# Sparse attention and a balanced mixture of experts on one core: the planner's durations, the first expert's w2 scale, and the sums of x

## The chip, the core and the metric

One core of one Trainium2 chip runs the whole program in one launch. The metric is the device time of one execution in microseconds, as a median of several runs. PE is the matmul engine (TensorE), DVE VectorE, ACT ScalarE, POOL GpSimd, and SP only issues DMAs. Each engine executes its own instructions in the order in which the program holds them; an instruction that waits holds up everything behind it on its engine.

## What is computed

```python
# attention: 4 batches x 8 heads, 768 positions, head size 64, block mask
scores = where(mask, q @ k.T / sqrt(64), -1e9); attn = softmax(scores); y = attn @ v
# x = y as [3072, 512]; 8 experts, w1 [8, 512, 1024], w2 [8, 1024, 512]
logits = x @ w_gate; P = exp(logits - logits.max())
for _ in range(8):
    P /= P.sum(1, keepdims=True) + 1e-9
    P /= P.sum(0, keepdims=True) + 1e-9
    P *= 3072 / 8
for e in range(8):
    out += P[:, e:e+1] * (relu(x @ w1[e]) @ w2[e])
```

## The kernel before

**Attention.** A table says after which of 192 tiles (one head, one 128-row column of keys) each step is issued; the order in it is kept on every engine. Batch 3 is the last. The first expert's w1 is loaded, scaled and split during attention. The load of the first w2 is issued at tile 184, and its scale is made at the very end of the table: eight sums of magnitudes on ACT (`magnitude`, L329), a maximum on DVE (L415), one transpose on PE that spreads it over the partitions (L335), and six short DVE steps (L421 to L428). The last two groups of transposes of the attention output (`turn_x`, L970) stand behind that PE transpose.

**Experts.** All 8 experts run over 4 batches, 32 rounds; round i is expert i // 4 and batch i % 4. A matmul of f32 accuracy is three f16 matmuls of high and low parts, so every operand is split: a high part by ACT and a low part by DVE or POOL. Both matrix products of a round use a seven-product (Strassen-like) scheme, p = 0 to 6. `stage1` multiplies by w1 (PE, L1546, 6 matmuls of 384 columns for each of four f-chunks of a product p), takes the results out of PSUM with ACT (L1528) and DVE (L1519), and forms the seven hidden operands h with POOL (L1784), ACT (L1746, L1761) and DVE or POOL (low parts, L1752 and L1750; L1767 on DVE). `stage2` multiplies by w2 (PE, L1866) and adds into acc with DVE (L1902). PE takes stage2 of round i and stage1 of round i + 1 in turn.

For the products p in `TWO = (6, 3, 1)` a second level of the scheme is used from expert 1 on (`inner_product`, L1575): 7 groups of 6 matmuls of 192 columns in place of 4 groups of 6 matmuls of 384. It needs sums of quarters of w1 (`inner` in `fetch_w1`, made on POOL L1299, ACT L1357, DVE L1362) and sums of quarters of x. The latter are made once for each batch and p, 12 times in all, by `prep_x`: load, add high and low part (L1482), four subtractions (L1491), split again (L1498, L1503), store to DRAM as `xsd`. Before, they are created in rounds 0 to 3, expert 0, and `closed[0]`, which every later use of the sums waits for, comes after the last of them.

**The planner.** `Plan` simulates the expert part before the program is emitted: each job has engines with durations, dependencies, buffers that it takes and drops, and a due time `dl` worked back from the jobs that need it. A job that may run on DVE or POOL goes to whichever the simulation would finish earlier. The simulation multiplies durations on ACT, DVE and POOL by `MARGIN`. What it yields is only an order: the program is emitted in the order in which the jobs start in the simulation, and semaphores do the rest. `balance` makes the eight normalisations of P: 8 chains of DVE steps (L1239 to L1260) with a PE matmul (L1250) in each.

**Memory.** `xfp` and `xst` (the f32 copy of x for odd batches, and four staging tiles) live in a 24 KB region until `close_late` releases it as a whole and the sums are put there.

Of the kernel before, what the change touches and what calls it, by code (L numbers as in the profile page):

```python
# [20 lines left out]
P = 128  # L21
# [14 lines left out]
SLK, SLK2, SHIFT, EASE = 1.5, 2.0, 8.0, 0.3  # L36
# [16 lines left out]
class Job:  # L53
    __slots__ = (
        "engs", "fn", "deps", "take", "drop", "pt", "dl", "stream", "kb",
        "rush", "wait", "succ", "start", "end", "eng", "ready", "seq", "free",
# [3 lines left out]
class Plan:  # L60
    LAT = 0.2
    DMA_RATE, DMA_LAND = 190.0, 2.0
    MARGIN = 1.06
# [21 lines left out]
    def job(self, engs, fn, deps=(), take=(), drop=(), pt=None, dl=None, stream=None, kb=0, rush=False):  # L85
# [7 lines left out]
        j.rush = rush  # L93
# [30 lines left out]
    def run(self):  # L124
# [3 lines left out]
        dma_free = 0.0  # L128
        items = {p: [(0.0, t) for t in ts] for p, ts in self.shelf.items()}
# [42 lines left out]
        def start(j, e, t):  # L172
            nonlocal dma_free, left
# [12 lines left out]
            else:  # L186
                j.end = t + dur
                free[e] = j.end
            if e == "-":
                free[e] = 0.0  # L190
# [7 lines left out]
            for s in j.succ:  # L198
                s.wait -= 1
                if not s.wait:  # L200
# [3 lines left out]
                    )  # L204
# [6 lines left out]
        while left:  # L211
            moved = False
            for e in ENG:
                while free[e] <= t + EPSI:
# [5 lines left out]
                    for j in mine:  # L220
                        if j.ready <= t + EPSI and allowed(j, t) <= t + EPSI:
# [33 lines left out]
            nxt = [free[e] for e in ENG if free[e] > t + EPSI]  # L255
            nxt += [j.ready for j in cand if j.ready > t + EPSI]
# [19 lines left out]
def tile_sparse_attention_moe(  # L276
# [79 lines left out]
    def scale_power(tag, s, inv, top):  # L356
# [10 lines left out]
    late = ExitStack()  # L367
    xfp, xst = (
        late.enter_context(tc.tile_pool(name=nm, bufs=n, side="right", reuse_waits="tile"))
        for nm, n in (("xfp", 1), ("xst", 4))  # L370
# [9 lines left out]
    def carve(at, dtype, *shape, home=arena):  # L380
# [9 lines left out]
        )  # L390

# [112 lines left out]
    def x_split(b, nm, at_):  # L504
        src = quads_of(b)[at_]
        st = xst.tile([P, 2, KH, TH], F16, tag="xs", name=f"xs_{b}_{nm}")
# [61 lines left out]
    with ExitStack() as actx:  # L568
# [18 lines left out]
        masks = xfp.tile([P, 2, S], BF16, tag="xf", name="masks")  # L587
# [377 lines left out]
        def turn_x(n, c0):  # L965
# [9 lines left out]
            if hp == 0 and c0 == 0:  # L975
                xfs[b] = (xfp if b % 2 else xfa).tile([P, KD, NC, P], F32, tag="xf", name=f"xf_{b}")
# [155 lines left out]
    sums = {}  # L1132

    shelf["xs"] = [xst.tile([P, 2, KH, TH], F16, tag="xs", name=f"stage_{n}") for n in range(4)]
# [12 lines left out]
    def ascend(b):  # L1147
# [21 lines left out]
        def plain(k):  # L1169
# [17 lines left out]
            pe = job({"PE": 1.0}, mm, los, take=(bk,), drop=free)  # L1187
# [33 lines left out]
    def balance(deps):  # L1221
# [9 lines left out]
        pe = job({"PE": 0.3}, spread, (d,), take=(b0,))  # L1231
# [5 lines left out]
        for it in range(8):  # L1237
            d = seq([
                ("DVE", 0.35, lambda: V.tensor_reduce(out=rs, in_=pw, axis=AX.X, op=ALU.add)),  # L1239
                ("DVE", 0.33, lambda: V.tensor_scalar(rs, rs, EPS, None, ALU.add)),  # L1240
# [10 lines left out]
                (d,), take=(bk,),  # L1251
# [7 lines left out]
                ("DVE", 0.29, lambda: V.tensor_scalar(cs, cs, CAP, None, ALU.mult)),  # L1259
# [13 lines left out]
    def scale_jobs(which, e, loaded):  # L1273
# [17 lines left out]
        pe = job({"PE": 0.3}, spread, (whole,), take=(bk,))  # L1291
# [31 lines left out]
    def fetch_w1(e):  # L1323
# [12 lines left out]
        d_s3 = tts(s3, q00, q10, KH, base, 1.3)  # L1336
        d_s1 = tts(q10, q10, q11, KH, tuple(d_s3), 1.35, ALU.add)
# [6 lines left out]
        def inner(p, src, deps):  # L1344
            if p not in TWO:
# [12 lines left out]
                (d, closed[0]) + tuple(used1.get((e - 1, p, "in"), ())),  # L1358
            )
            lo = job(  # L1360
                {"DVE": 1.5},
# [13 lines left out]
        d_s2 = tts(q00, q10, q00, KH, tuple(out[0]) + tuple(d_s1), 1.35)  # L1375
        put(5, q00, d_s2)
        d_s4 = tts(q00, q01, q00, KH, tuple(out[5]), 1.35)
# [7 lines left out]
    def fetch_w2(e, loaded=None, done=None):  # L1385
# [8 lines left out]
        if loaded is None:  # L1394
            loaded = raw_load(2, e)
# [15 lines left out]
        d_t1 = tts(t1, m01, m00, h2, base, 0.85)  # L1411
        one = put(1, m10, base)
        zero = put(0, m00, d_t1)
        d5 = tts(m00, m11, t1, h2, tuple(zero), 1.05)
        five = put(5, m00, d5)
        d6 = tts(m01, m01, m11, h2, tuple(d_t1), 1.05)
        six = put(6, m01, d6)
        d3 = tts(m10, m10, m00, h2, tuple(one) + tuple(d5), 1.05)
# [31 lines left out]
    def load_x(i):  # L1450
# [6 lines left out]
        if i >= B:  # L1457
            for p in TWO:
# [4 lines left out]
                        deps + (closed[0],),  # L1463
# [3 lines left out]
    def prep_x(i):  # L1467
        b = i % B
        for p in TWO:
# [11 lines left out]
                {"DVE": 0.95, "POOL": 2.1},  # L1481
# [6 lines left out]
            for o, x, y in ((0, 1, 0), (1, 3, 1), (3, 3, 0), (2, 2, 3)):  # L1488
                last = job(
                    {"DVE": 0.36, "POOL": 0.75},  # L1490
# [22 lines left out]
                384, (lo,), drop=(st,),  # L1513
# [18 lines left out]
    def stage1(i, t0, length):  # L1532
        e, b = divmod(i, B)
        two = TWO if e else ()
# [142 lines left out]

        got = {}
        if two:
            got[6] = inner_product(6)  # L1680
            got[3] = inner_product(3, got[6])
            got[1] = inner_product(1)

        for g in range(NF // 2):
# [3 lines left out]
            if two:  # L1688
                R, U, C = got[1][0][g], got[6][0][g], got[3][0][g]
                rdep, udep, cdep = (  # L1690
                    [x for k in range(2) for x in got[p][1][g, k]] for p in (1, 6, 3)
                )
                t_r = t_u = t_c = ()
            else:
                R, U, C = (hold("pair") for _ in range(3))
# [19 lines left out]
            if two:  # L1715
                for q, (j, end) in outer(0, X, True, {}).items():
                    r_[q] = scaled_add(cell(R, q), bank(X[q]), cell(R, q), [j] + rdep, dl=end + SLK)
                for q, (j, end) in outer(5, X, False, {q: (r_[q],) for q in qis}).items():
                    c_[q] = scaled_add(cell(C, q), bank(X[q]), cell(C, q), [j] + cdep, dl=end + SLK)
                for q, (j, end) in outer(4, X, False, {q: (c_[q],) for q in qis}).items():  # L1720
                    u_[q] = scaled_add(cell(U, q), bank(X[q]), cell(U, q), [j] + udep, dl=end + SLK)
            else:
                Z = {q: hold("s1") for q in qis}
                Y = {q: hold("s1") for q in qis}
                first = lambda t, q: (t,) if q == qis[0] else ()
                k0, k5, k6 = {}, {}, {}
                for q, (j, end) in outer(0, X, True, {}).items():
                    k0[q] = scaled_copy(cell(R, q), bank(X[q]), (j,), take=first(R, q), dl=end + SLK)
                for q, (j, end) in outer(1, Z, True, {}).items():
                    r_[q] = scaled_add(cell(R, q), bank(Z[q]), cell(R, q), (j, k0[q]), drop=(Z[q],), dl=end + SLK)  # L1730
                for q, (j, end) in outer(5, X, False, {q: (k0[q],) for q in qis}).items():
                    k5[q] = scaled_copy(cell(C, q), bank(X[q]), (j,), take=first(C, q), dl=end + SLK)
                for q, (j, end) in outer(6, Y, True, {}).items():
                    k6[q] = scaled_copy(cell(U, q), bank(Y[q]), (j,), take=first(U, q), dl=end + SLK)
                for q, (j, end) in outer(4, X, False, {q: (k5[q],) for q in qis}).items():
                    u_[q] = scaled_add(cell(U, q), bank(X[q]), cell(U, q), (j, k6[q]), dl=end + SLK)
                for q, (j, end) in outer(3, Y, False, {q: (k6[q],) for q in qis}).items():
                    c_[q] = scaled_add(cell(C, q), bank(Y[q]), cell(C, q), (j, k5[q]), drop=(Y[q],), dl=end + SLK)
# [263 lines left out]
```

## Time and profile before

| | |
|---|---|
| time, median of 3 runs | 2198.71 us (2198.5 to 2200.9) |
| profiled execution, its own time | 2204.29 us |
| its span, first to last instruction | 2202.5 us |
| mean granted PE clock | 0.990 |
| busy PE / DVE / ACT / POOL | 2131.7 / 1740.9 / 1357.3 / 1575.0 us |

The span has three parts: attention up to about 423 us, expert 0 up to about 657 us (where the first second-level matmul stands), and experts 1 to 7. PE's busy time counts a matmul in the slow clock state as busy, so a loss of PE time is the idle time and, beside it, the share of the clock that was not granted.

### The profile page before, as it was taken

Reading aid. Unit: us, or ns where it says so; the run is one execution under the profiler, and the core shown is the slowest. Engines: PE = TensorE matmul, PEld = TensorE weight load, DVE = VectorE, ACT = ScalarE, POOL = GpSimd, SP = SyncE. Lnnn points to the kernel's source line nnn. Section 1 sums busy time; section 2 is a strip of 40 time slices with the busy share of each in tenths; the row PEclk is TensorE's granted clock in tenths of the full one; section 3 lists DMA queues with packets and bytes.
Section 4 is the critical chain, followed back from the end, with each engine's and each line's share of the span. In section 5 each row is a group of like instructions: output and inputs, shape, how many; then the busy total and the mean of one; then the engine's idle time right before and its main releaser. Section 6 shows DMA issues by size and latency. Waiting matters only on the chain.

```text
span 2202.5 us, 50394 instructions
## 1 busy us (share of the span) xinstructions
PE 2131.7 (97%) x20404; PEld 1699.5 (77%) x20404; DVE 1740.9 (79%) x2835; ACT 1357.3 (62%) x2570; POOL 1575.0 (72%) x1602
## 2 busy tenths in 40 slices
PE   6999999799989999999999999999999999999999
PEld 3777676567668888888888888888888888888887
DVE  8878888599997877787778787878787877688766
ACT  4788878776556666655565556545655566556543
POOL 5556668587676876877788678868876877687654
PEclk9999999999999999999999999999999999999999
DMA  7667856434544533554454445443554345444421
GB/s 169 141 145 156 204 124 138 143 104 130 165 158 139 197 128 127 174 182 130 134 167 165 137 137 168 163 149 115 168 182 144 118 151 191 135 139 149 148 87 65
DMA packets 226526, 323.11 MB, mean 147 GB/s; under 512 B 135132, under 2 KB 153588, under 8 KB 226292
## 3 DMA queue, kind: packets, MB, share of 16 engines
q1 hardware_dynamic: 225728, 319.86, 48.0%
q8 instruction: 159, 2.61, 0.5%
q14 instruction: 75, 0.61, 0.1%
q10 hardware_dynamic: 564, 0.03, 0.0%
HBM read 222.33 MB, written 66.06 MB: 131 GB/s over the span
## 4 chain that ended last, share of the span: by engine, by line
PE 75%; DVE 9%; POOL 9%; issue 3%; ACT 2%; DMA 2%; SPq 0%; DVEq 0%; POOLq 0%; ACTq 0%
PE y L1866 31%; PE p L1546 19%; PE p L1575 12%; POOL r L1299 4%; PE u L939 4%; POOL u L1784 3%; PE t L877 2%; PE m L841 2%; PE m L844 2%; PE t L874 2%; DVE h L1752 2%; POOL h L1750 1%; DVE top L850 1%; DMA qt<-qs 1%; DVE stage L1491 1%
## 5 line engine op out<-in xcount | busy, mean ns | idle before, releaser
L1866 PE MATMUL y<-w2p,h 128*128 128x256 f16 x8064 | 973.9, 273 | 2.9 <-DVE acc L1902 2.8
L1866 PEld LDWEIGHTS <-h 128*128 128x128 f16 x8064 | 787.8, 98 | 122.0 <-issue 3.6
L1750 POOL TENSOR_TENSOR h<-pair,h 128x384 f16<-128x384 f32 x294 | 306.0, 1053 | 278.7 <-ACT h L1761 262.8
L1902 DVE SCALAR_TENSOR_TENSOR acc<-y,spare,acc 128x256 f32<-128x256 f32 (+1 forms) x588 | 302.4, 517 | 170.9 <-PE y L1866 168.1
L1761 ACT ACTIVATE h<-pair 128x384 f16<-128x384 f32 x640 | 321.0, 518 | 137.1 <-POOL pair L1784 66.1
L1784 POOL TENSOR_TENSOR u<-u,pair 128x384 f32<-128x384 f32 x256 | 306.0, 1211 | 64.7 <-ACT u L1528 47.9
L1519 DVE SCALAR_TENSOR_TENSOR pair<-p,pair 128x384 f32<-128x384 f32 x384 | 212.4, 555 | 137.7 <-PE p L1546 136.0
L1546 PE MATMUL p<-attic 128*128 128x384 f16 x1632 | 296.6, 326 | 3.5 <-DVE pair L1519 3.5
L1546 PE MATMUL p<-arena 128*128 128x384 f16 x1632 | 293.9, 327 | 0.0
L1528 ACT ACTIVATE u<-p 128x384 f32<-128x384 f32 x296 | 142.7, 487 | 201.7 <-PE p L1575 108.3
L1746 ACT ACTIVATE pair<-pair 128x384 f32<-128x384 f32 x384 | 194.2, 516 | 102.6 <-DVE pair L1519 93.0
L1546 PEld LDWEIGHTS <-attic 128*128 128x128 f16 x1728 | 169.6, 98 | 98.0 <-issue 5.2
L1546 PEld LDWEIGHTS <-arena 128*128 128x128 f16 x1632 | 159.7, 98 | 89.8 <-issue 1.4
L850 DVE TENSOR_REDUCE top<-m 128x1 f32<-128x768 f32 x192 | 182.0, 951 | 54.2 <-PE m L844 53.3
L882 ACT ACTIVATE pe<-t,qk 128x768 int32<-128x768 f32 x192 | 172.3, 899 | 72.9 <-PE t L877 65.5
L1752 DVE SCALAR_TENSOR_TENSOR h<-pair,h 128x384 f16<-128x384 f32 x218 | 198.4, 924 | 9.5 <-ACT h L1761 9.4
L1575 PEld LDWEIGHTS <-sums 128*128 128x128 f16 x2016 | 174.6, 98 | 18.8 <-issue 14.0
L1299 POOL TENSOR_TENSOR r<-r 128x256 f32<-128x256 f32 (+1 forms) x162 | 172.1, 1078 | 8.3 <-DVE pair L1646 2.9
L1575 PE MATMUL p<-xs,sums 128*128 128x192 f16 x1512 | 161.8, 247 | 10.1 <-ACT u L1528 7.6
L1784 POOL TENSOR_TENSOR pair<-pair,pair 128x384 f32<-128x384 f32 x128 | 155.3, 1231 | 1.5 <-ACT pair L1746 1.5
L896 POOL TENSOR_SCALAR pl<-pe 128x768 f16<-128x768 uint16 x112 | 96.6, 866 | 76.2 <-ACT pe L882 71.1
L1784 POOL TENSOR_TENSOR pair<-u,pair 128x384 f32<-128x384 f32 x128 | 146.3, 1162 | 0.3
(220 smaller groups left out, 3697.5 us busy)
## 6 DMA issues: line engine op xcount, KB each, us to landing
arena<-xd SPq DMA_DIRECT2D x128, 384.0 KB, 3.2
accd<-acc SPq DMA_DIRECT2D x56, 768.0 KB, 4.0
acc<-accd SPq DMA_DIRECT2D x56, 768.0 KB, 5.3
attic<-xd SPq DMA_DIRECT2D x96, 384.0 KB, 3.4
r<-in_moe_w_dram SPq DMA_DIRECT2D x16, 2048.0 KB, 9.1
xs<-xsd SPq DMA_DIRECT2D x84, 384.0 KB, 3.9
arena<-in_q_dram SPq DMA_DIRECT2D x16, 384.0 KB, 4.0
arena<-in_k_dram SPq DMA_DIRECT2D x16, 384.0 KB, 4.6
```

Of the source, the lines that this page charges most:

```text
L850: nc.vector.tensor_reduce(out=tops[n][:, c : c + 1], in_=sc[:, :S], axis=AX.X, op=ALU.max)
L1299: lambda: nc.gpsimd.tensor_tensor(out=out(), in0=x(), in1=y(), op=op), deps,
L1519: lambda: nc.vector.scalar_tensor_tensor(out=out_(), in0=bank_(), scalar=HDOWN, in1=add(), op0=ALU.mult, op1=ALU.add),
L1546: nc.tensor.matmul(bk.tile[:, :TH], lhsT=w1p[p][:, l, kc, fs], rhs=xp[p][:, r, kc], start=(fresh and kc == 0 and m == 0), stop=(kc == KH - ...
L1575: nc.tensor.matmul(bk.tile[:, c * HT : (c + 1) * HT], lhsT=lhs(l, c), rhs=rhs(rr), start=(fresh and c == 0 and m == 0), stop=(m == 2), ski ...
L1746: return job({"ACT": 0.52}, lambda: nc.scalar.activation(view(), view(), AF.Relu), dep)
L1750: nc.gpsimd.tensor_tensor(out=out_, in0=x, in1=y, op=ALU.subtract)
L1752: nc.vector.scalar_tensor_tensor(out=out_, in0=x, scalar=1.0, in1=y, op0=ALU.mult, op1=ALU.subtract)
L1761: lambda: nc.scalar.activation(h.tile[:, 0], src(), AF.Relu if relu else AF.Copy),
L1784: lambda: nc.gpsimd.tensor_tensor(out=o(), in0=x(), in1=y(), op=op), deps, **kw
L1866: nc.tensor.matmul(py, lhsT=hh[i, p, kc].tile[:, l, tsl], rhs=w2p[p][:, r, kc], start=(old is None and kc == 0 and m == 0), stop=(kc == h2 ...
L1902: lambda dst=dst, src=src, t=t: nc.vector.scalar_tensor_tensor(out=dst(), in0=src(), scalar=pwe[e][:, t : t + 1] if e else 1.0, in1=dst(), ...
```

## The change

- The scale of the first w2 leaves the table of attention and becomes planned jobs (`scale_jobs`), placed among the work of stage1 of round 0.
- In expert 1 only p = 1 is made by the second level (`TWO1`); p = 6 and 3 join in expert 2. `prep_x` is created for one batch and p at a time, with due times: p = 1 at 50 to 170, p = 6 and 3 at 190 to 310 of the plan's time. `closed` becomes one condition for each p.
- The first two of the four subtractions of `prep_x` become one instruction over two slots.
- The 24 KB region is one tile, `loft`, from which the masks, the f32 x, the staging tiles and the sums are carved; nothing is released as a whole.
- `MARGIN` goes from 1.06 to 1.0, and many durations are replaced. PE jobs in the balance chain, the logits and the spread of scales get a `lag`: the plan takes them as ready 1 or 2 us later than their input. The weights of expert 0 get a due time (`SOON`). `port` and `SLK3` are added and used by no job.

```diff
-    MARGIN = 1.06
+    MARGIN = 1.0
...
                     s.ready = max(
...
-                    )
+                    ) + s.lag
...
         def start_w2():
             load_w(2, 0)
-            parts, whole, spread, power = scale_steps(2, 0)
-            for n, part in enumerate(parts):
-                at(NTILE + n // 4, LATER, part)
-            at(NTILE + 2, LATER, whole)
-            at(NTILE + 2, LAST, spread)
-            at(NTILE + 3, LATER, power)
...
-        pe = job({"PE": 0.3}, spread, (whole,), take=(bk,))
+        pe = job({"PE": 0.3}, spread, (whole,), take=(bk,), lag=2.0)
...
             pe = job(
                 {"PE": 0.4},
                 lambda bk=bk: nc.tensor.matmul(bk.tile[:, :NE], lhsT=ones, rhs=cs, start=True, stop=True),
-                (d,), take=(bk,),
+                (d,), take=(bk,), lag=2.0,
...
-                {"DVE": 0.95, "POOL": 2.1},
+                {"DVE": 1.19, "POOL": 2.3},
...
-            for o, x, y in ((0, 1, 0), (1, 3, 1), (3, 3, 0), (2, 2, 3)):
+            last = job(
+                {"DVE": 0.92, "POOL": 1.1},
+                lambda i0=wide(1, 2), i1=wide(0, 1): plan.engine(nc).tensor_tensor(
+                    out=i1(), in0=i0(), in1=i1(), op=ALU.subtract
+                ),
+                (last,),
+            )
+            for o, x, y in ((3, 3, 0), (2, 2, 3)):
                 last = job(
-                    {"DVE": 0.36, "POOL": 0.75},
+                    {"DVE": 0.88, "POOL": 0.72},
...
-                        {"DVE": 0.65, "POOL": 1.02},
+                        {"DVE": 0.92, "POOL": 1.08},
                         lambda: low(h.tile[:, 1], src(), h.tile[:, 0]), (hi,), drop=drop,
...
-        two = TWO if e else ()
+        two = twos(e)
...
-        if two:
+        one, many = 1 in two, 6 in two
+        if many:
             got[6] = inner_product(6)
             got[3] = inner_product(3, got[6])
+        if one:
             got[1] = inner_product(1)
...
+    def twos(e):
+        return () if e == 0 else TWO1 if e == 1 else TWO
...
+    for n in range(B):
+        for p in TWO1:
+            prep_x(n, p, PREP0 + PREPD * n)
+    for n in range(B):
+        for p in TWO:
+            if p not in TWO1:
+                prep_x(n, p, PREP1 + PREPD * n)
+    for p in TWO:
+        closed[p] = rest if p in TWO1 and TWO != TWO1 else rest + tuple(xprep.values())
...
     weight_job(0, (even,))
-    late_users = list(stored.values()) + list(keeps)
+    weighed[0].dl = SOON
```

## Rows read from the trace of the kernel before

**Rows 1.** Engines by stretch: us, busy of PE, PEld, DVE, ACT, POOL; PEclk, DMA, GB/s.
```profile
424.00:431.00 7.00, 0.48 (x1) 0.18 (x1) 0.47 (x3) 5.68 (x16) 5.44 (x8) 0.61 0.00 2
...
433.20:439.40 6.20, 6.20 (x33) 3.40 (x32) 2.94 (x4) 5.17 (x9) 0.00 (x0) 0.79 0.33 127
```

**Rows 2.** Engines by longer stretches of the expert part, same columns.
```profile
433.20:467.90 34.70, 34.70 (x236) 20.72 (x235) 26.92 (x32) 27.48 (x53) 22.57 (x21) 0.96 0.35 103
...
478.00:628.00 150.00, 141.96 (x1102) 105.53 (x1100) 137.76 (x204) 93.14 (x203) 108.83 (x92) 0.99 0.46 149
628.00:678.00 50.00, 39.72 (x320) 32.90 (x319) 42.34 (x63) 25.34 (x46) 42.97 (x39) 0.86 0.50 173
678.00:903.00 225.00, 222.87 (x1973) 184.78 (x1971) 180.91 (x310) 143.13 (x291) 162.47 (x151) 1.00 0.45 151
```

**Rows 3.** What PE waited for, 430 to 700 us: total, times, longest.
```profile
PE u L335 <- DVE ma_w L415: 7.6, 1, 7.6
PE p L1250 <- DVE spare L1244: 6.2, 3, 3.5
PE p L1575 <- ACT u L1528: 4.0, 1, 4.0
PE p L1546 <- DVE pair L1519: 3.5, 1, 3.5
PE y L1866 <- DVE acc L1902: 2.8, 1, 2.8
```

**Rows 4.** What PE waited for, 678 us to the end.
```profile
PE p L1575 <- DVE u L1617: 4.0, 6, 1.1
PE p L1575 <- ACT u L1528: 3.6, 5, 1.4
```

**Rows 5.** Timeline, all engines, at the end of attention: start, duration, instruction.
```profile
423.06 0.56 DVE L960 TENSOR_TENSOR xn<-u,r 128x384 f32<-128x384 f32 x1
423.89 0.63 ACT L329 ACTIVATE unread<-r 128x512 bf16<-128x512 f32 x1 [2.66 <-DMA r<-in_moe_w_dram]
...
429.93 0.16 DVE L415 TENSOR_REDUCE ma_w<-mx_w 128x1 f32<-128x8 f32 x1 [6.32 <-ACT unread L329]
```

**Rows 6.** Timeline of PE from the end of attention on.
```profile
431.01 0.90 PE L970 MATMUL u<-ident,xn 128*128 128x128 f32 x3 [0.39 <-DVE ma_w L421]
...
433.19 6.34 PE L1546 MATMUL p<-arena 128*128 128x384 f16 x30
439.36 0.17 PE L1178 MATMUL p<-gh,stage 128*128 128x8 f16 x1
...
443.34 6.01 PE L1546 MATMUL p<-attic 128*128 128x384 f16 x36
449.19 6.01 PE L1546 MATMUL p<-arena 128*128 128x384 f16 x36
```

**Rows 7.** Timeline of PE in expert 1, second-level matmuls.
```profile
669.70 1.15 PE L1575 MATMUL p<-attic 128*128 128x192 f16 x12
670.69 1.15 PE L1575 MATMUL p<-xs,sums 128*128 128x192 f16 x12
```

**Rows 8.** Timeline of DVE just before the 3.5 us wait.
```profile
633.06 3.17 DVE L1491 TENSOR_TENSOR stage<-stage 128x192 f32<-128x192 f32 x4
636.16 1.01 DVE L1519 SCALAR_TENSOR_TENSOR pair<-p,pair 128x384 f32<-128x384 f32 x2
```

**Rows 9.** Groups of DVE, 425 to 700 us: busy, mean ns, idle before.
```profile
L1491 DVE TENSOR_TENSOR stage<-stage 128x192 f32<-128x192 f32 x32 | 28.0, 875 | 1.7 <-POOL stage L1491 1.0
...
L1503 DVE TENSOR_TENSOR stage<-stage,stage 128x768 f16<-128x768 f32 x10 | 12.6, 1259 | 0.1
L1482 DVE TENSOR_TENSOR stage<-stage 128x768 f32<-128x768 f16 x10 | 11.9, 1188 | 0.3 <-DMA stage<-xd 0.3
```

**Rows 10.** Groups, whole span: the DVE takings-out from PSUM.
```profile
L1519 DVE SCALAR_TENSOR_TENSOR pair<-p,pair 128x384 f32<-128x384 f32 x384 | 212.4, 555 | 137.7 <-PE p L1546 136.0
```

**Rows 11.** One line's instructions, whole span: shortest, median, longest ns.
```profile
L1752 DVE SCALAR_TENSOR_TENSOR h<-pair,h x218: 541/873/2165, 447.9 to 2176.1; 128x384 f16<-128x384 f32 x109
```

More of the change, by code (lines that the diff above doesn't have):

```diff
@@ L55 @@
         "engs", "fn", "deps", "take", "drop", "pt", "dl", "stream", "kb",
-        "rush", "wait", "succ", "start", "end", "eng", "ready", "seq", "free",
+        "rush", "lag", "port", "wait", "succ", "start", "end", "eng", "ready", "seq", "free",
     )
@@ L366, in tile_sparse_attention_moe @@
     raw = ctx.enter_context(tc.tile_pool(name="raw", bufs=1))
[L367 to L370, printed above, removed]
+    loft = ctx.enter_context(tc.tile_pool(name="loft", bufs=1, side="right")).tile(
+        [P, 24 * 256], F32, name="loft"
     )
@@ L390, in carve @@
         )
+    stages = [carve((12 + 3 * n) * 1024, F16, 2, KH, TH, home=loft) for n in range(4)]
+    turned = [0]
     wr = {}
@@ L505, in x_split @@
         src = quads_of(b)[at_]
-        st = xst.tile([P, 2, KH, TH], F16, tag="xs", name=f"xs_{b}_{nm}")
+        st = stages[turned[0] % 4]
+        turned[0] += 1
         nc.scalar.activation(st[:, 0], src, AF.Copy)
@@ L586, in tile_sparse_attention_moe @@
         fence = aconst.tile([P, NB], BF16, name="fence")
-        masks = xfp.tile([P, 2, S], BF16, tag="xf", name="masks")
+        masks = carve(0, BF16, 2, S, home=loft)
         onehot = masks[:, 0]
@@ L975, in turn_x @@
             if hp == 0 and c0 == 0:
-                xfs[b] = (xfp if b % 2 else xfa).tile([P, KD, NC, P], F32, tag="xf", name=f"xf_{b}")
+                if b % 2:
+                    xfs[b] = carve(0, F32, KD, NC, P, home=loft)
+                else:
+                    xfs[b] = xfa.tile([P, KD, NC, P], F32, tag="xf", name=f"xf_{b}")
             nc.scalar.activation(
@@ L1131, in tile_sparse_attention_moe @@
     xsd = [dram.tile([P, NP, 2, 4, TH // 2], F16, name=f"xsd_{b}") for b in range(B)]
-    sums = {}
-    shelf["xs"] = [xst.tile([P, 2, KH, TH], F16, tag="xs", name=f"stage_{n}") for n in range(4)]
+    shelf["xs"] = stages
     plan = Plan(shelf)
@@ L1186, in plain @@
             free = tuple(parts[j][0] for j in range(2))
-            pe = job({"PE": 1.0}, mm, los, take=(bk,), drop=free)
+            pe = job({"PE": 1.0}, mm, los, take=(bk,), drop=free, lag=1.0)
             keep = job(
@@ L1687, in stage1 @@
             bank = lambda bk: (lambda: bk.tile[:, :TH])
[L1688 to L1695, printed above, removed]
+            made = lambda p: (got[p][0][g], [x for k in range(2) for x in got[p][1][g, k]])
+            R, rdep = made(1) if one else (hold("pair"), [])
+            C, cdep = made(3) if many else (hold("pair"), [])
+            U, udep = made(6) if many else (hold("pair"), [])
             cell = lambda t, q: (lambda: t.tile[:, q % 2])
@@ L1713, in outer @@
                 return res
-            if two:
-                for q, (j, end) in outer(0, X, True, {}).items():
+            first = lambda t, q: (t,) if q == qis[0] else ()
+            prior = {}
+            for q, (j, end) in outer(0, X, True, {}).items():
+                if one:
                     r_[q] = scaled_add(cell(R, q), bank(X[q]), cell(R, q), [j] + rdep, dl=end + SLK)
-                for q, (j, end) in outer(5, X, False, {q: (r_[q],) for q in qis}).items():
-                    c_[q] = scaled_add(cell(C, q), bank(X[q]), cell(C, q), [j] + cdep, dl=end + SLK)
[L1720 to L1731, printed above, removed]
@@ new lines, in stage1 @@
+                    prior[q] = (r_[q],)
+                else:
+                    k = scaled_copy(cell(R, q), bank(X[q]), (j,), take=first(R, q), dl=end + SLK)
+                    prior[q] = (k,)
+            if not one:
+                Z = {q: hold("s1") for q in qis}
+                for q, (j, end) in outer(1, Z, True, {}).items():
+                    r_[q] = scaled_add(
+                        cell(R, q), bank(Z[q]), cell(R, q), (j,) + prior[q], drop=(Z[q],), dl=end + SLK
+                    )
@@ L1732, in stage1 @@
+            if not many:
+                Y = {q: hold("s1") for q in qis}
+            k5, k6 = {}, {}
+            for q, (j, end) in outer(5, X, False, prior).items():
+                if many:
+                    c_[q] = scaled_add(cell(C, q), bank(X[q]), cell(C, q), [j] + cdep, dl=end + SLK)
+                    k5[q] = c_[q]
+                else:
                     k5[q] = scaled_copy(cell(C, q), bank(X[q]), (j,), take=first(C, q), dl=end + SLK)
+            if not many:
                 for q, (j, end) in outer(6, Y, True, {}).items():
@@ L1951, in tile_sparse_attention_moe @@
         more = i + 1 < NI
-        s1 = (S1A if (i + 1) // B == 0 else S1B) if more else 0.0
-        length = S2 + s1
-        if TWO and i < B:
-            prep_x(i)
-            late_users += [xprep[i, p] for p in TWO]
-        if i == B - 1:
-            closed[0] = job({"-": 0.0}, close_late, tuple(late_users))
+        length = S2 + (spent1((i + 1) // B) if more else 0.0)
         if more:
```

107 lines of the change are left out of this document (61 added, 46 removed).

## The prediction

> **What bounds the kernel now.** The page's first part comes first: PE is busy 97% of the span, the others 62 to 79%. So time can go only where PE idles, runs in its slow clock state, or has fewer matmuls, and the views to read are PE's waits and the granted clock by stretch.
>
> The waits say where. From 430 to 700 us the five largest add up to 24.1 us [rows 3]; from 678 us to the end, 1525 us, the two largest add up to 7.6 us, none of them over 1.4 [rows 4]. Experts 1 to 7 are bound by the matmuls themselves; what can be won lies between the end of attention and the start of expert 1, in three places.
>
> The first is one wait of 7.6 us on DVE's L415 [rows 3]. The timeline shows its cause: ACT starts the eight magnitudes of w2 at 423.89, when their load lands, and DVE can form the maximum only at 429.93 [rows 5]. PE's transpose L335 waits for it, and the `turn_x` transposes behind it start at 431.01 though their input was ready at 423.06 + 0.56 = 423.62 [rows 5, 6]. In the wait the granted clock falls: it is 0.61 over 424 to 431 and still 0.79 over 433.2 to 439.4, where PE is never idle [rows 1]. A level between 0.5 (1.2 GHz) and 1 (2.4 GHz) is a mixture of the two.
>
> The second is 478 to 628 us: PE idles 150 − 141.96 = 8.0 us with the clock at 0.99 [rows 2], and 6.2 us of it are three waits of the balance chain's matmul for DVE [rows 3]. DVE is busy 137.76 of 150 there [rows 2], so the chain's steps come later than planned while PE's place in the order is fixed.
>
> The third is 628 to 678 us: PE idles 50 − 39.72 = 10.3 us at a mean clock of 0.86 [rows 2], which is another 50 × 0.14 = 7.0 us not granted: 17.3 us lost in 50. Its waits are the other three [rows 3]. Ahead of the 3.5 us one, DVE runs four subtractions of `prep_x` back to back for 3.17 us while a taking-out from PSUM waits behind them [rows 8]. The plan counted 0.36 × 1.06 = 0.38 us for each; 32 of them took 875 ns on average [rows 9].
>
> **The change part by part.** The sum is made against the profiled execution, 2204.29 us, which is 5.58 above the median of the runs (2198.71); I take the same distance off at the end.
>
> *A, the w2 scale leaves the end of attention.* The `turn_x` transposes can start at about 423.7 in place of 431.01: 7.3 us. Then the clock: the first 30 matmuls of stage1 take 439.36 − 433.19 = 6.17 us; at the later rate, 36 in 449.19 − 443.34 = 5.85 or 0.1625 each, they need 4.88 [rows 6]. Without the long wait that is 1.3 us more. Together −8.6; bounds −7.3 (the clock falls anyway) and −9.4 (the slow transposes gain as well, at most half of 0.90 for each of two groups [rows 6], so 0.8 taken).
>
> *B, the balance chain.* With `lag` the plan puts its PE matmuls 2 us later behind their input. The three waits average 2.1 us, the longest is 3.5 [rows 3], so most of each goes. Lost now: 8.0 idle and about 150 × 0.01 = 1.5 of clock [rows 2], 9.5 in all. The chain now has an early due time, so its DVE steps come in front of takings-out. I keep 2 us of loss: −7.5, bounds −3 (only half of the 6.2) and −9.5.
>
> *C, the sums of x.* Twelve preparations cost DVE 28.0 + 12.6 + 11.9 = 52.5 us [rows 9]. Eight of them, about 35 us, have due times after expert 0, and two thirds of the weight sums of expert 1 vanish. Taken from the 137.76 + 42.34 = 180.1 us that DVE is busy over 478 to 678 [rows 2], 35 leave 145 of 200, or 73%. The plan also counts 0.88 us where it counted 0.38, so what remains stands at truer places. Against it: expert 1's stage1 now begins with product 1, whose weight sums are the last that `fetch_w1` makes, behind a chain of four POOL sums and their splits. stage2 of round 3 can fill PE meanwhile. I keep 4 of the 17.3 us: −13, bounds −6 (only the waits of 3.5 and 2.8 go [rows 3]) and −17.
>
> *D, expert 1 with one second-level product.* For each of p = 6 and 3 and each of four batches, 24 matmuls of 0.1625 us [rows 6] take the place of 42 of (670.69 − 669.70) / 12 = 0.0825 [rows 7]: 3.90 − 3.47 = 0.43, times 8: +3.5. This is nearly certain, since PE is the bound there.
>
> *E, where the scale goes.* The magnitudes are 429.93 − 423.89 = 6.0 us of ACT [rows 5] and fall into the stretch that is now 433.2 to 467.9, where ACT is busy 27.48 of 34.7 [rows 2]: 33.5 of 34.7 then. POOL's first w2 sums, made before 431 with PE idle [rows 1], move behind them too. Stage2 of round 0 may start late; PE has stage1 of round 1 to do meanwhile. If that cover is gone the price is the whole 6.0; below nothing it can't be. I take +2.
>
> *F, what expert 1 receives.* Of DVE's 180.91 us in 678 to 903 [rows 2], the first-level form frees ten takings-out a batch (25 with three second-level products, 15 with one) at 0.555 us [rows 10]: −22 us over four batches; 35 us of preparations come in. That is 194 of 225, and POOL and ACT have 62 and 82 us free. Some chains will be late: +1, bounds 0 and +4.
>
> *G, the other durations.* MARGIN falls to 1.0 and single durations rise: a low part on DVE counts 0.92 in place of 0.65 × 1.06 = 0.69, and took 0.541 to 2.165 with a median of 0.873 [rows 11]; a taking-out counts 0.56 in place of 0.594 and took 0.555 [rows 10]. The plan gets truer in the mean and loses its slack for scatter. From 678 us on there are only some 8 us of waits to win [rows 4]; I take +1, bounds −6 and +10.
> The low parts spread from 0.54 to 2.17 us, while takings-out, with one operand in PSUM, stay at 0.555 [rows 10, 11]. The Trainium skill, "GPSIMD Engine Reference", section Key points, says that GpSimd shares its SBUF interfaces with VectorE and contends with DVE instructions that read two SBUF inputs; these rows agree. It speaks against this change, since the new figures (0.92 against 1.08) send more low parts to POOL than 0.65 against 1.02 did: by it I would put G at +4 as an estimate, and the sum 3 us higher.
>
> *The edits that cost nothing*: the DMA loads and stores of `prep_x` keep their number, and the `loft` views hold the same bytes as the pools. SP is not on PE's path while a load is ready ahead of use; if the carved tile brought a wait that the pools did not have, it would be paid once at 423 us, in A. The spread's PE transpose (a few tenths) is only moved.
>
> Sum: −8.6 − 7.5 − 13 + 3.5 + 2 + 1 + 1 = −21.6, so 2204.3 − 21.6 = 2182.7 for such an execution, and 2198.7 − 21.6 = **2177** for the median.
>
> **The rivals.**
> - *Product 1 comes late* (0.20). The stall at the start of expert 1 stays with another name: PE waits for the sums of w1 for p = 1, and C gives 5 in place of 13. For it: PE did wait 4.0 us in this very place for its first second-level results [rows 3]. Against it: 4 + 4 of POOL's sums are gone from in front. Time 2185.
> - *ACT becomes the bound of round 0* (0.12). From 33.5 of 34.7 us on, every further delay shows: E is 6 and takes B's start with it, some 2 more. So the wait of A goes on as a wait for h or for w2's splits. Time 2177 + 6 = 2183.
> - *A better order everywhere* (0.15). The waits of [rows 4] go and the boundary between experts 0 and 1 is as smooth as the others: G at −3, C at −15. Time 2171.
> - *The plan without slack* (0.08). Slower. Each round has 25 + 12 takings-out, 28 rounds 1036 of them. The 21.6 us are gone if they hold up PE by 21 ns each on average. If every tenth comes 0.5 us late, behind a low part that took 1.4 and not 0.92 us, it is 52 us: time 2229; at half of that 2203. For it: the spread of [rows 11]. Against it: with durations for low parts that were too short by a quarter the plan lost hardly anything after 678 us [rows 4].
> - *No change* (0.03): A wins 8.6, and C and B give half of that back by new waits. Time 2199.
>
> **How the numbers follow.** My forecast has 0.42. The bounds of A to G, taken as independent, spread it by some ± 8; with the rivals on both sides the range that holds 8 in 10 is 2164 to 2191. About 0.2% (4.4 us) is what a measurement here can tell from no change. The first four cases are faster: 0.89, of which I leave 0.02 to mishaps; 0.04 the same; 0.09 slower.
>
> **What would show it.** Right: no wait at L335 before 433, the first stage1 matmul at about 425.5 with the clock near 1; no wait over 1.5 us at L1250; L1491 instructions after 660 us; 192 more L1546 matmuls and 336 fewer L1575; stage2's first matmul about 7 us earlier than the end of the first stretch of [rows 2]. Wrong: PE waits of several us around 455 to 465 (E), around 640 to 660 for ACT or DVE (C), or many short ones for DVE spread over experts 2 to 7 (G), in which case the forecast fails by its sign.

## The result and the profile after

The kernel after takes 2178.63 us (median of 4 runs, 2177.97 to 2181.63) against 2199.65 before (4 runs, 2198.5 to 2200.9): ratio 0.9907, interval 0.989 to 0.9924, so 21.0 us less. The forecast was 2177 in 2164 to 2191. The total came out as forecast; three of its terms (A, B and G) were not worth what it gave them, and the experiments show why, as far as it is known.

The profiled execution of after took 2179.01 us with a span of 2177.2, 25.3 less than before's. Of these, 4.6 us belong to no part of the change: the last attention output is ready at 423.62 us before [rows 5] and at 418.40 + 0.56 = 418.96 after, and over the profiles of this study, all with the same attention, that moment lies between 416.1 and 423.6. So stretches are compared here by their distance from the first stage1 matmul.

What PE waited for in after, from 415 to 700 us (total, times, longest), against [rows 3]:

```profile
PE p L1564 <- DVE pair L1537: 7.4, 1, 7.4
PE p L1564 <- DVE spare L1263: 5.2, 3, 1.8
PE u L982 <- DVE xn L972: 1.1, 1, 1.1
...
PE u L982 <- ACT loft L992: 0.6, 1, 0.6
```

The wait for the w2 scale is gone, and so are those for ACT and DVE at the start of expert 1. Line numbers have moved: stage1's matmul is L1564 (was L1546), its second level L1593 (L1575), the taking-out L1537 (L1519). The chain's matmul L1258 (L1250) waits for nothing any more; but a stage1 matmul now waits 5.2 us for L1263, the chain's own reading of its bank, and there is a new wait of 7.4 us.

Timeline of PE at the end of attention, against [rows 6]:

```profile
419.02 0.55 PE L982 MATMUL u<-ident,xn 128*128 128x128 f32 x3 [1.08 <-DVE xn L972]
420.14 0.55 PE L982 MATMUL u<-ident,xn 128*128 128x128 f32 x3 [0.58 <-ACT loft L992]
420.52 5.04 PE L1564 MATMUL p<-arena 128*128 128x384 f16 x30
425.40 0.17 PE L1186 MATMUL p<-gh,loft 128*128 128x8 f16 x1
```

Stage1 begins 420.52 − 418.96 = 1.56 us after the last output, where it was 433.19 − 423.62 = 9.57, and its first 30 matmuls take 425.40 − 420.52 = 4.88 us, not 6.17.

Windows of after; the second to fourth are those of [rows 2] moved by 12.7 us, the distance of the first stage1 matmuls:

```profile
420.50:425.40 4.90, 4.90 (x32) 2.95 (x31) 3.00 (x5) 4.64 (x10) 0.00 (x0) 1.00 0.34 132
...
465.30:615.30 150.00, 136.61 (x1029) 101.43 (x1027) 130.58 (x206) 93.29 (x198) 127.76 (x109) 0.97 0.40 129
615.30:665.30 50.00, 50.00 (x406) 38.87 (x405) 37.82 (x47) 34.82 (x76) 48.56 (x44) 1.00 0.51 171
665.30:890.30 225.00, 220.44 (x1814) 173.30 (x1813) 156.88 (x242) 145.36 (x293) 183.30 (x172) 1.00 0.45 153
...
538.40:547.00 8.60, 1.23 (x7) 0.68 (x7) 8.43 (x12) 2.12 (x4) 7.37 (x6) 0.74 0.37 130
547.00:553.00 6.00, 6.00 (x24) 3.34 (x23) 4.63 (x9) 0.74 (x2) 1.08 (x2) 0.52 0.45 126
...
1000.00:2100.00 1100.00, 1097.04 (x9718) 911.05 (x9716) 798.67 (x1328) 634.97 (x1300) 888.86 (x865) 1.00 0.46 151
```

The stretch into expert 1 lost 17.3 us of 50 before and now has PE busy in all 50 at clock 1.00. The stretch of the balance chain has become worse: 13.4 us idle at 0.97, against 8.0 at 0.99. And experts 2 to 7, from 1000 to 2100 us, idle 3.0 us; the same window of before idles 7.2:

```profile
1000.00:2100.00 1100.00, 1092.84 (x9643) 904.36 (x9641) 851.45 (x1406) 632.26 (x1290) 828.87 (x768) 1.00 0.45 149
```

For a ledger, what PE lost in a stretch is its length less its matmuls, each at its time in undisturbed stretches (0.161 us for 384 columns, 0.082 for 192, 0.108 for 256 in stage2). Idle time and clock are both in it. "Gap" is from the last attention output to the first stage1 matmul, the columns behind it us after that matmul. The last column has a constant part (PE's last matmul ends some 4 us before the span does, in every kernel).

| kernel | gap | 0–110 | 110–190 | 190–250 | 250–430 | rest |
|---|---|---|---|---|---|---|
| before | 9.6 | 7.3 | 9.4 | 17.2 | 4.1 | 29.9 |
| after | 1.5 | 8.7 | 13.0 | 0.4 | 4.7 | 24.8 |
| difference | −8.1 | +1.4 | +3.6 | −16.8 | +0.6 | −5.1 |

These add up to −24.4; with the added matmuls (+3.5) and the scatter of attention (−4.6) that is −25.5, against 25.3 measured.

The new wait, first on PE and then on DVE:

```profile
535.49 0.28 PE L1258 MATMUL p<-spare,ones 128*128 128x8 f32 x2
...
538.39 1.14 PE L1564 MATMUL p<-arena 128*128 128x384 f16 x6 [1.63 <-DVE spare L1263]
546.89 4.00 PE L1564 MATMUL p<-arena 128*128 128x384 f16 x12 [7.37 <-DVE pair L1537]
```

```profile
539.18 1.11 DVE L1268 TENSOR_TENSOR pw<-pw,spare 128x192 f32<-128x192 f32 x1
540.22 1.66 DVE L1521 TENSOR_TENSOR loft<-loft 128x768 f16<-128x768 f32 x1
541.80 0.34 DVE L1247 TENSOR_REDUCE spare<-pw 128x24 f32<-128x192 f32 x1
542.06 1.75 DVE L1490 TENSOR_TENSOR loft<-loft 128x768 f32<-128x768 f16 x1
543.85 1.15 DVE L1501 TENSOR_TENSOR loft<-loft 128x384 f32<-128x384 f32 x1
545.03 1.34 DVE L1509 TENSOR_TENSOR loft<-loft 128x192 f32<-128x192 f32 x2
546.29 0.55 DVE L1537 SCALAR_TENSOR_TENSOR pair<-p,pair 128x384 f32<-128x384 f32 x1
```

DVE runs one step of the chain, the end of one preparation (L1521), another step, and the first four instructions of the next preparation (L1490 to L1509), and only then the taking-out that frees PE's bank.

### The profile page after: what moved, and what is told of

It is laid out like the page before. It is cut to its first block, busy times and chain, and to the rows that moved or that the text cites. A ratio compares the mean times of both kernels' runs of the same rounds, so it can differ in the third digit from the quotient of the medians.

```text
span 2177.2 us, 50086 instructions
## 1 busy us (share of the span) xinstructions
PE 2121.5 (97%) x20260; PEld 1685.4 (77%) x20260; DVE 1622.7 (75%) x2641; ACT 1358.9 (62%) x2584; POOL 1666.8 (77%) x1734
## 4 chain that ended last, share of the span: by engine, by line
PE 84%; POOL 7%; DVE 5%; issue 1%; ACT 1%; DMA 1%; SPq 0%; POOLq 0%; ACTq 0%; DVEq 0%
PE y L1894 35%; PE p L1564 24%; PE p L1593 11%; PE u L951 4%; POOL r L1307 3%; PE t L886 2%; PE t L889 2%; PE m L853 2%; PE m L856 2%; POOL u L1812 1%; POOL h L1778 1%; DVE top L862 1%; DMA qt<-qs 1%; POOL pair L1812 1%; PE u L982 0%
## 5 line engine op out<-in xcount | busy, mean ns | idle before, releaser
L1778 POOL TENSOR_TENSOR h<-pair,h 128x384 f16<-128x384 f32 x384 | 390.2, 1032 | 223.5 <-ACT h L1789 204.1
L1812 POOL TENSOR_TENSOR u<-u,pair 128x384 f32<-128x384 f32 x256 | 291.7, 1151 | 60.3 <-ACT u L1546 53.5
L1564 PE MATMUL p<-attic 128*128 128x384 f16 x1728 | 315.5, 326 | 0.0
L1537 DVE SCALAR_TENSOR_TENSOR pair<-p,pair 128x384 f32<-128x384 f32 x384 | 212.1, 555 | 138.6 <-PE p L1564 135.7
L1564 PE MATMUL p<-arena 128*128 128x384 f16 x1632 | 293.9, 327 | 10.8 <-DVE pair L1537 7.4
L1546 ACT ACTIVATE u<-p 128x384 f32<-128x384 f32 x284 | 137.1, 487 | 234.0 <-PE p L1593 141.5
L1564 PEld LDWEIGHTS <-attic 128*128 128x128 f16 x1920 | 187.9, 98 | 105.8 <-issue 1.9
L1564 PEld LDWEIGHTS <-arena 128*128 128x128 f16 x1632 | 159.7, 98 | 101.0 <-issue 13.1
L1307 POOL TENSOR_TENSOR r<-r 128x256 f32<-128x256 f32 (+1 forms) x158 | 165.5, 1063 | 19.7 <-DVE arena L1324 8.7
L1778 POOL TENSOR_TENSOR h<-u,h 128x384 f16<-128x384 f32 x156 | 166.9, 1087 | 0.2 <-ACT h L1789 0.2
L1593 PEld LDWEIGHTS <-loft 128*128 128x128 f16 x1824 | 157.5, 98 | 9.6 <-issue 5.5
L1546 ACT ACTIVATE pair<-p 128x384 f32<-128x384 f32 x132 | 64.2, 488 | 140.5 <-DVE acc L1930 65.1
L1593 PE MATMUL p<-loft 128*128 128x192 f16 x1368 | 145.5, 246 | 4.3 <-ACT u L1546 3.9
L1812 POOL TENSOR_TENSOR pair<-pair,pair 128x384 f32<-128x384 f32 x128 | 149.0, 1179 | 0.0
```

The costliest lines, as they stand in the source:

```text
L1307: lambda: nc.gpsimd.tensor_tensor(out=out(), in0=x(), in1=y(), op=op), deps,
L1537: lambda: nc.vector.scalar_tensor_tensor(out=out_(), in0=bank_(), scalar=HDOWN, in1=add(), op0=ALU.mult, op1=ALU.add),
L1546: lambda: nc.scalar.activation(out_(), bank_(), AF.Relu if relu else AF.Copy, scale=HDOWN),
L1564: nc.tensor.matmul(bk.tile[:, :TH], lhsT=w1p[p][:, l, kc, fs], rhs=xp[p][:, r, kc], start=(fresh and kc == 0 and m == 0), stop=(kc == KH - ...
L1593: nc.tensor.matmul(bk.tile[:, c * HT : (c + 1) * HT], lhsT=lhs(l, c), rhs=rhs(rr), start=(fresh and c == 0 and m == 0), stop=(m == 2), ski ...
L1778: nc.gpsimd.tensor_tensor(out=out_, in0=x, in1=y, op=ALU.subtract)
```

## The experiments

All ratios are to before, with before run on the same chip. The rounds were on different chips, and before's median in them lies between 2199.65 and 2202.2 us, so times of different rounds that lie less than some 3 us apart can't be told from each other.

**Later due times for the preparations.** After, with one edit:

```diff
-            prep_x(n, p, PREP0 + PREPD * n)
+            prep_x(n, p, 130.0 + 15.0 * n)
```

> The kernel after with the preparations of x for p = 1 due at 130 to 175 of the plan's time in place of 50 to 170. Theory 1: the 7.4 us wait of PE for a taking-out at 539 to 547 us is there because preparations that are past their due time go ahead of the taking-out on DVE; then the wait goes with the slow clock behind it (lost in that stretch: 9.0 idle and 3.3 of clock), and the time is 2167 to 2170. Theory 2: DVE has simply too much to do in 480 to 550 us, late or not; then the same loss stands elsewhere in expert 0, and the time is 2176 to 2180.

2171.93 us, 0.9872 (0.9858 to 0.9885): 6.7 us below after, and with `no_lag` below the fastest kernel here; theory 1 holds, though the time is 2 us above its range. The stretch from 528 to 553 us, which holds the new wait in after, has PE busy throughout:

```profile
528.00:553.00 25.00, 25.00 (x197) 18.97 (x195) 23.08 (x44) 16.90 (x35) 23.20 (x21) 1.00 0.41 127
```

In after the same 25 us hold 16.00 us of PE at a clock of 0.80. DVE is busier here (23.08 against 22.63), but with takings-out between the preparations. The loss in the column 110–190 falls from 13.0 to 1.0.

**No due time for the weights of expert 0.** After, without `weighed[0].dl = SOON`, which is what makes the chain early.

> The kernel after without the due time of the weights of expert 0, so that the balance chain's steps on DVE are no longer urgent. If it is the chain (some 25 us of DVE steps squeezed into 70 us) that makes DVE late for takings-out and for itself, the three waits of PE for the chain (5.2 us) and the 7.4 us wait go: 2165 to 2168. If the chain only pays for its own waits and the preparations cause the other: 2172 to 2175, with the 7.4 us wait still there. If the lag was what shortened the waits and the due time does nothing: 2178.

2176.73 us, 0.9894 (0.988 to 0.9907): 1.9 below after, inside the intervals. The 7.4 us wait is gone (0.9 lost in 110–190), but 13.8 are lost in 0–110 and 5.8 in 190–250 (after: 8.7 and 0.4). So the early chain is one of the two things that make that wait, and doing without the due time only moves the loss.

**No lag.** After, without the four `lag=` arguments.

> The kernel after without any lag. If the lag is what keeps PE from waiting for the balance chain, the waits of L1258 and of the matmuls behind it grow from 5.2 us to 8 or more and the time to 2181 to 2185. If the chain's waits come from DVE being late by its own order, nothing changes beyond 2 us: 2177 to 2180.

2173.7 us, 0.9871 (0.9855 to 0.9887): 4.9 below after, the opposite of what I expected of it. From 412 to 700 us the chain's matmul waits little:

```profile
PE p L1258 <- DVE spare L1252: 2.0, 3, 0.7
```

Neither the wait for L1263 nor the one of 7.4 us stands in that list, and 110–190 loses 1.0. So `lag` is not what cured the waits of the chain. What it did is seen where the chain (L1263, once in each of its eight turns) and the preparations (their first step, L1490) stand, in after and then without the lag:

```profile
L1263 DVE TENSOR_SCALAR spare<-p x8: 148/154/167, 482.5 to 568.7; 128x8 f32<-128x8 f32 x8
L1490 DVE TENSOR_TENSOR loft<-loft x12: 946/1582/2019, 533.6 to 717.2; 128x768 f32<-128x768 f16 x12
```

```profile
L1263 DVE TENSOR_SCALAR spare<-p x8: 150/152/168, 480.8 to 536.7; 128x8 f32<-128x8 f32 x8
L1490 DVE TENSOR_TENSOR loft<-loft x10: 940/1321/2017, 541.0 to 716.4; 128x768 f32<-128x768 f16 x10
```

Without the lag the chain is through before the first preparation begins. With it, the chain reaches 35 us into the preparations, and that is where the new wait stands.

**The scale back in attention's table.** After, with part A undone (the removed `scale_steps` lines of the diff put back, `fetch_w2(0, started)`).

> The kernel after with the first w2's scale back in the table of attention, all else as after. Theory (the parts are not additive): before, DVE had the last word up to the start of expert 1, so starting earlier gained nothing; after, PE has it, so the 8 us of wait and 1.3 of clock come back in full: 2187 to 2189. Rival: the 7.4 us wait of expert 0 is there because round 0 starts earlier, and goes when it starts later: 2179 to 2182.

2179.91 us, 0.9901 (0.9888 to 0.9915): 1.3 above after, which can't be told from it (by the ratios, 0.9901 against 0.9907, it is even the lower). The waits from 412 to 700 us:

```profile
PE u L345 <- DVE ma_w L426: 7.9, 1, 7.9
PE p L1569 <- DVE spare L1269: 3.1, 2, 1.9
```

The old wait is back, with a gap of 9.9 us, and the 7.4 us wait is not there (0.9 lost in 110–190). The move wins its 8 us, and in this version of the order nearly all of it is spent again 120 us later.

**The move alone.** Before, with part A and nothing else.

> The kernel before with one part of the change alone: the first w2's scale becomes planned jobs. If the 7.6 us wait of PE's transpose is all there is to it, the first stage1 matmul starts about 1.6 us after the attention output is ready and not 9.6 us, and the clock stays up: about 8 + 1.3 less, 2190 to 2191. If the 6 us of ACT that move into round 0 are paid there (rival), a PE wait of several us appears between 440 and 480 us and the time is 2195 to 2199.

2207.8 us, 1.0031 (1.002 to 1.0043): slower by 7, where every reading had it faster. The gap is 1.5 us here too, but PE waits elsewhere, from 412 us to the end:

```profile
PE p L1570 <- ACT u L1523: 7.6, 10, 3.2
PE y L1861 <- DVE acc L1897: 7.2, 3, 6.5
PE y L1861 <- DVE w2p L1310: 6.1, 3, 3.2
PE p L1244 <- DVE spare L1238: 4.8, 1, 4.8
```

Against before it loses 12.8 for 9.4 in 110–190, 13.5 for 4.1 in 250–430 and 37.3 for 29.9 in the rest. The time won at the end of attention is still there when expert 1 begins (its first second-level matmul stands 226.5 us after the last attention output, 233.2 before), and is lost behind it.

**The durations alone.** Before, with `MARGIN = 1.0` and the new durations.

> The kernel before with MARGIN 1.0 and the new durations alone; no lag, no due times, four single subtractions counted at 0.88, w2's scale in attention. If the durations are worth about 8 us in experts 2 to 7, as the kernel after with the old ones suggests, and little in expert 0, where DVE is full whatever the plan knows: 2189 to 2195, with fewer waits at the starts of experts 2 to 7. If their worth depends on the other parts: 2198 to 2204.

2183.26 us, 0.992 (0.9905 to 0.9936): far more than any reading gave it. Its waits from 412 to 700 us:

```profile
PE u L335 <- DVE ma_w L415: 7.5, 1, 7.5
PE p L1546 <- DVE pair L1519: 4.3, 1, 4.3
```

The chain's waits of [rows 3] are gone without `lag` and without the spread: 1.0 is lost in 110–190, where before lost 9.4. In 190–250 it still loses 12.9. From 1000 to 2100 us PE idles 3.3:

```profile
1000.00:2100.00 1100.00, 1096.66 (x9700) 909.51 (x9698) 800.75 (x1332) 634.14 (x1303) 884.20 (x858) 1.00 0.46 151
```

**The old durations.** After, with `MARGIN = 1.06` and every duration as before.

> The kernel after with MARGIN and all durations as before (the new two-slot subtraction counts 0.62 on DVE); where jobs are created, their due times and the lags stay. If what removed the stall of expert 0 to 1 is that eight preparations and two sets of weight sums left the stretch, the time stays within 3 us of 2178.6. If it is that the plan now counts the real durations, waits of PE for DVE of 2 to 4 us come back between 480 and 700 us and the time is 2185 to 2195.

2186.69 us, 0.9937 (0.9924 to 0.9951): 8.1 above after, as expected in size but not in place. The loss is in the rest (36.0 against 24.8), not between 480 and 700 us; from 1000 to 2100 us PE idles 10.3:

```profile
1000.00:2100.00 1100.00, 1089.70 (x9626) 902.67 (x9624) 842.47 (x1385) 631.78 (x1290) 845.29 (x790) 1.00 0.45 150
```

**Which of the durations.** Before, first with `MARGIN = 1.0` alone, then with this and the low parts:

```diff
-                        {"DVE": 0.65},
+                        {"DVE": 0.76},
...
-                        {"DVE": 0.65, "POOL": 1.02},
+                        {"DVE": 0.92, "POOL": 1.08},
```

> The kernel before with MARGIN 1.0 and every duration as it was. If what made the plan truer is that the 6% on takings-out and splits went, most of the 17 us of the durations come here: 2183 to 2190. If it is the low parts and preparations, which were counted too short, that matter, MARGIN alone makes them shorter still: 2200 to 2210, with more waits of PE for DVE.

> The kernel before with MARGIN 1.0 and the durations of the h low parts alone (DVE 0.92 and POOL 1.08 in place of 0.65 and 1.02; 0.76 in place of 0.65 for L1767). If the low parts are what the plan had wrong, 2183 to 2190, and POOL does some 100 of them more than before (254 then). If the preparations were: within 4 us of the run with MARGIN alone.

2216.75 us, 1.0076 (1.0061 to 1.0091), and 2195.1 us, 0.9977 (0.9968 to 0.9986). The margin alone costs 17 us; the three figures for low parts win 21.7 on top of it, of the 33.5 by which `durations_only` lies below the margin alone. Windows of the two kernels, the margin alone first:

```profile
1000.00:2100.00 1100.00, 1087.57 (x9610) 900.83 (x9608) 854.90 (x1392) 627.81 (x1277) 831.14 (x769) 1.00 0.45 150
```

```profile
1000.00:2100.00 1100.00, 1089.51 (x9605) 901.62 (x9604) 783.83 (x1302) 631.79 (x1290) 888.04 (x867) 1.00 0.45 149
```

The low parts take 71 us off DVE and put 57 on POOL. POOL makes 549 of 768 of them here, against 401 in before (the 254 in the expectation is a miscount) and 410 with the margin alone. In this window that wins only 1.9 us of idle time (12.4 to 10.5); the larger part is won earlier, in the columns 0–110 (22.8 to 10.3) and 190–250 (13.1 to 9.5).

**The durations and the move.** Before, with `durations_only` and part A together.

> The kernel before with the new durations and the planned scale of w2, without due times, lags and the new spread of the sums. If starting stage1 8 us earlier pays as soon as the plan counts the real durations: 2174 to 2177 (9 less than with the durations alone, 2183.3). If it pays only once the sums are spread, because DVE still decides when expert 1 can start: 2181 to 2186, with more than 15 us lost between 110 and 250 us behind the first stage1 matmul.

2194.11 us, 0.9973 (0.9963 to 0.9983): some 11 us slower than the durations alone. From 600 to 860 us:

```profile
PE p L1570 <- ACT u L1523: 7.3, 2, 5.2
PE y L1861 <- DVE acc L1897: 5.6, 1, 5.6
PE y L1861 <- DVE h L1762: 4.8, 2, 4.6
```

The gap is 1.5 us, but 22.6 are lost in 190–250, where the durations alone lost 12.9. All twelve sums of x have to be ready there, and the move brings that stretch 8 us nearer; that this is the cause is argued, not shown.

**All three second-level products in expert 1.** After, with `TWO1 = TWO`: the moves and durations stay, the spread goes.

> The kernel after with all three second-level products in expert 1, so that all 12 preparations must be done before it; the durations, lags and the planned scale stay. Matmuls alone would give 3.5 us back, 2175. Theory: DVE and POOL can't do the preparations and three sets of weight sums before expert 1, and PE waits there for some 10 to 17 us with its clock: 2185 to 2193. Rival: true durations alone are enough to place the work, the stall is under 4 us: 2175 to 2179.

2191.84 us, 0.9956 (0.9943 to 0.9968): 13.2 above after, though it saves the 3.5 us of added matmuls. The 60 us that hold the start of expert 1:

```profile
608.10:668.10 60.00, 49.72 (x411) 40.24 (x409) 50.85 (x60) 33.54 (x62) 54.89 (x46) 0.91 0.56 186
```

15.5 us are lost in 190–250, against 0.4 in after. The spread is what clears the boundary.

## Why the prediction was right, and where its steps were not

- **A, the w2 scale**: right in place and size for the gap (−8.1, and the 30 matmuls 6.17 to 4.88 us, together −9.4 against −8.6), wrong as a term that can be added. Undoing it in after changes nothing that can be told (+1.3 us). The three kernels that end the 7.4 us wait by a due time or the lag, with A kept, lie lower than the kernel with A undone, by 3.2 (`no_due`), 6.2 (`no_lag`) and 8.0 us (`prep_late`); A undone in one of these was not run. Alone on before A costs 7, on the durations 11. The step that failed is the silent one that the 8 us stay won: stage1 starts earlier, and PE waits later, 120 us on in after, around the start of expert 1 on the durations, mostly behind it on before. That DVE then still owes the same work is the likely reason; it is not shown for all three.
- **B, the balance chain** (−7.5): this step failed. The column 110–190 lost 3.6 us more, and the stretch that the forecast went by (478 to 628 us, 465.3 to 615.3 in after) idles 13.4 us for 8.0. `lag` does put the chain's matmul behind its input (no wait, against 2.0 us in `no_lag`), but that isn't PE time won: the stage1 matmul behind it waits 5.2 us for L1263 instead. The kernel without `lag` is 4.9 us faster, and there the chain is through before the preparations begin; the durations alone take the chain's waits off the list. My sentence "its DVE steps come in front of takings-out" was the right warning with the wrong price, 2 us for a wait of 7.4 and a slow stretch after it. I had the preparations in mind as gone from this stretch. Those for p = 1 have due times in it, so preparations and the chain's steps both stood ahead of a taking-out. That making either of the two later, or the chain shorter, ends this wait is shown (`prep_late`, `no_due`, `no_lag`); why the plan put them so is argued from the code, where the earliest due time goes first.
- **C, the sums of x** (−13): right that spreading the sums clears the boundary (`three_at_once`); 16.8 where I kept 13 of 17.3. The working behind it was not right, and that the size fits is in part luck. I let eight preparations leave expert 0 and DVE's busy time fall from 180.1 to 145 of 200 us. But the due times of p = 6 and 3 begin at 190, and expert 1's first second-level matmul comes 208 us after the first stage1 matmul: seven of the twelve L1490 start before it, so five left, and DVE is busy 130.58 + 37.82 = 168.4 us there. The rival "product 1 comes late" fell: PE is busy in all 50 us of that stretch.
- **D, fewer second-level matmuls**: as worked out. L1564 has 3552 matmuls where L1546 had 3360, and L1593 has 3192 where L1575 had 3528: 192 more and 336 fewer.
- **E, where the scale goes** (+2): nothing in stage2's start. Its first matmul comes 454.62 − 420.52 = 34.1 us after that of stage1, 34.7 before [rows 2]; the whole column 0–110 grew by 1.4, though A's clock gain of 1.3 is in it; 3.5 us of the waits for L1263 lie there. ACT was no bound in round 0, and that rival fell with its wait.
- **F, what expert 1 receives** (+1): +0.6.
- **G, the durations** (+1, bounds −6 and +10): sign and size failed. In the ledger the rest is −5.1; in the kernel they are worth 8.1, on before 17 (in both cases the margin and the figures together; the margin alone costs 17 on before). I looked for their gain only among the waits after 678 us and saw some 8 us there, which was right for experts 2 to 7. But the same figures also decide the order in expert 0, and the waits of the chain that I gave to `lag` were theirs.

The sum was right partly by luck, because errors went against each other: B 11 us too good, C 4 and G 6 us too bad. The rival "better order everywhere" is what happened outside of the chain's stretch; the rival "without slack" exists for the margin alone (2216.75), and it is the truer figures for low parts that more than pay for it.

The contention rule that I weighed under G (the Trainium skill, "GPSIMD Engine Reference", section Key points) did not decide against the change. What I feared by it did happen, 139 more low parts went to POOL (401 to 540 of 768); but in 1000 to 2100 us DVE's busy time fell by 53 us, POOL's rose by 60, and PE's idle time fell from 7.2 to 3.0. The low parts that stayed on DVE, shortest, median and longest in ns, against [rows 11]:

```profile
L1780 DVE SCALAR_TENSOR_TENSOR h<-pair,h x128: 543/774/1998, 451.8 to 2154.9; 128x384 f16<-128x384 f32 x128
```

These are one of two forms, and so was [rows 11]: the other (h<-u) has a median of 1116 for 954, and over both the mean is 0.94 us before and after. The low parts on DVE got fewer and not shorter, and PE did not pay for the scatter that is still there.

**Left open.** `prep_late` and `no_lag` each take away the same wait; what they give together is open. A kernel with both in smaller form (lags of 1 us, later due times) took 2174.61 us, but it does not compute the reference's output, and why is open, so its time settles nothing. The new durations with the margin of 1.06 were not run. Why A costs 7 to 11 us where the sums of x are not spread is located (experts 1 to 7 on before, the start of expert 1 on the durations) but not taken apart. So are the differences in experts 2 to 7 between kernels that differ only ahead of them: `no_lag` idles 8.0 us from 1000 to 2100 us, after 3.0.

## What to carry to other kernels

In a program whose order comes from a planner, a part that is moved must be priced with what it pushes: ask which short job on the busiest helper engine will stand behind the moved ones, and whether their due times fall into the same stretch. Durations measured in the running kernel can be worth as much as a change of structure (17 of 2200 us here; two thirds of what the figures won, 21.7 of 33.5 us, came from those for one short job that may run on DVE or POOL), so try them alone first. And take parts out of the final version as well as adding them to the old one: A costs 7 or 11 us, or changes nothing that can be told, by the company it has.

## What the runs showed of the hardware

After the idle stretch of 538.4 to 547.0 us (PE busy 1.23 of 8.60, granted clock 0.74), the clock is 0.52 over the next 6 us although PE is busy in all of them: about the lower of the two levels, 1.2 GHz. So the wait of 7.4 us cost 6 × 0.48 = 2.9 us more behind it. In before, the 7 us wait was followed by 6.2 us at 0.79 [rows 1].

The same DVE instruction scatters widely: L1263 to L1268, four steps on at most 192 columns, have the same order in `after` and in `prep_late`, and L1268 takes 1.11 us in the one (539.18) and 0.36 in the other (at 540.92 and at 549.51). The traces show what sets it: whether POOL is inside an instruction when the step starts (in `prep_late` POOL's next one begins at 549.52, just behind the step of 549.51). POOL in after, then a step of the same size on DVE while POOL idles:

```profile
538.01 2.07 POOL L1812 TENSOR_TENSOR pair<-u,pair 128x384 f32<-128x384 f32 x2
542.96 2.80 POOL L1778 TENSOR_TENSOR h<-u,h 128x384 f16<-128x384 f32 x2
551.84 1.26 POOL L1509 TENSOR_TENSOR loft<-loft 128x192 f32<-128x192 f32 x2 [6.07 <-DVE loft L1501]
```

```profile
548.49 0.36 DVE L1250 TENSOR_TENSOR pw<-pw,spare 128x192 f32<-128x192 f32 x1
```

The L1268 of 539.18 starts inside POOL's second L1812 and ends at 540.29, 0.21 us after it (540.08). Over the whole of after, the 28 low parts (L1780) with no POOL instruction beside them took 0.544 to 0.553 us. The 175 that started with over 0.1 us of a POOL instruction to go took a median of 1.115, and nine in ten of them ended 0.414 to 0.420 us after that instruction. So these steps, with both operands in SBUF, waited for POOL's instruction to end. The takings-out, with one operand in PSUM, did not: a median of 0.557 us with POOL at work, 0.558 without, and a mean of 0.551 to 0.556 in every profile here. A single duration for such a job in the plan stands for the mean of these waits; `port`, which the change adds and no job uses, would let the plan hold one such job back while another runs.
